# Linear attention, a mixer and a spectral layer on one core: packed copies on SyncE, transposed keys shared between head pairs, and a new written order

## The chip, the core and the metric

The kernel runs on one core of one Trainium2 chip. The metric is the device time of one execution in microseconds (us), from the runs of the program; lower is better. A core has five engines that each run their own instructions in order: TensorE (PE in the profile, with its weight loads as PEld), VectorE (DVE), ScalarE (ACT), GpSimd (POOL) and SyncE (SP), which here issues most transfers. Transfers (DMAs) can be issued by SP, by ACT and by POOL; the profile shows an issue as SPq, ACTq or POOL.

## The reference: what is computed

Three layers follow each other, with B = 4 batches, H = 8 heads, S = 768 tokens, D = 48 per head, and 384 channels.

```python
for t in range(S):                                                       # attention, per batch and head
    state = alpha[:, :, t, :, None] * state + k[:, :, t] (outer) v[:, :, t]
    y[:, :, t] = q[:, :, t] @ state
h = x.T @ U @ V;  u = x + h.T                                            # mixer, rank 32, over tokens
x1 = u + relu(u @ w_ch1) @ w_ch2                                         # 384 -> 1536 -> 384
theta = x1 @ w_theta;  zr, zi = x1 * cos(theta), x1 * sin(theta)         # spectral layer
u = x1 + w_tok_r @ zr + w_tok_i @ zi                                     # 768 x 768 over tokens
out = u + relu(u @ w_ch)
```

The recurrence is computed in chunks of C = 128 tokens (NC = 6 of them): keys and queries are scaled by running products of the decays, the part within a chunk is a masked product of scores and values, and the state between chunks comes from a scan.

## The kernel before, in words

**Layout.** The 384 channels of a batch lie in KD = 3 tiles of 128 rows. A tile i < 3 holds two whole heads (rows 0 to 47 and 64 to 111) and, in rows 48 to 63 and 112 to 127, 16-row pieces of heads 2 and 5 (`ROWS`). Those two heads make the fourth pair (p = 3, `PAIRS[3]`): its keys, queries and decay products are packed out of the three tiles by small transfers, and its results are put back into their rows of X.

**Attention.** `att_load` (SP) loads decays, keys, queries and values. `prep_k` and `prep_q` scale: a DVE scan G (line 247), a product for the keys (249), a second scan (257), a product for the queries (258), and the decay product tp of a chunk (279). `spread` (letter R) calls `spare` (line 239), which packs 16-row pieces of scaled keys into kp and of queries into qp; ACT issues these. `att_pe(b, p)` then makes one pair in eight steps: `across` (transposes of the keys, line 322, copied to kt by ACT, 323), `scores` for two halves (302, with a mask by ACT and POOL, 308 and 309, or by DVE, 312), `increments` (333), `states` (ACT spreads tp into tb, 340, DVE scans into S, 344), `within` (354), `before` (362, copied to X by ACT, 364), and for p = 3 the return of the pieces to X by SP (412).

**Mixer.** Batch 0 goes by `rank_columns` (letters 0, 1, 2; transposes in line 475), the others by `rank` (K; 429, 420). `lift` makes u, split in high and low parts, `expand` and `contract` (M and N, the two halves of the tokens) are the 384-1536-384 layer with three products per tile (598 to 600). The weights arrive as 64-bit words and are decoded by DVE in three passes (`conv`, 511, 514, 517; letters U for U and V, L for w1 and w2, T for the second layer's).

**Spectral layer.** `theta` (H) makes angles, sines and cosines; `factors` (V) and `sums` (S) make the operands of seven token products (terms 2, 1, 6, 7, 5, 3, 4), some of the sums by accumulating transfers from POOL (`plus`, 828); `products7` (G, line 898) makes the products in groups of six matmuls (mx), and adds them to xq (903, 905) after a term's last group; `operands` (Y) and `outputs` (C) end it. `layers`, `back` (X), `squared` (Q, which checks the decays on ACT), `loads` (D), `preps` (P) and `checked` (F) are the other generators; A and B are `products` for even and odd pairs.

**What sets the order.** Everything is issued in a written order: the text `ORDER` is read letter by letter, and each letter runs its generator to its next yield. A generator that needs something not made yet runs the other generator first. The order of the instructions of one engine is the order in which they were issued this way. The strings `BY_K` to `BY_U` say for each of many products, splits and masks whether DVE (V) or POOL (P), or for `BY_A` DVE or ACT with POOL (A), makes it. Tiles in SBUF are `SLOTS` = 61 slots of 128 x 768 words, taken and given back in the written order; PSUM has 8 banks handled alike.

```python
    for x in "".join(ORDER.split()):
        next(gens[x], None)
```

## Time and profile before

| | |
|---|---|
| time, median of 3 runs | 692.6 us (690.29 to 693.17) |
| profiled execution: its own time | 692.24 us |
| profiled execution: span from first to last instruction | 690.5 us |
| mean granted clock of TensorE | 0.984 of full |
| transfers | 71.89 MB, 104 GB/s on the mean |

The span is what the rows below divide. "Busy" is the time in which an engine has at least one instruction running; matmuls overlap each other, so their mean duration is longer than the step from one to the next. "Idle before" and "waits" name what ended a stretch in which an engine had nothing running; a time in square brackets is such a stretch. All window and timeline times count from the start of the span.

### The profile page before, as it was taken

Reading aid. Unit: us, or ns where it says so; the run is one execution under the profiler, and the core shown is the slowest. Engines: PE = TensorE matmul, PEld = TensorE weight load, DVE = VectorE, ACT = ScalarE, POOL = GpSimd, SP = SyncE. Lnnn points to the kernel's source line nnn. Section 1 sums busy time; section 2 is a strip of 40 time slices with the busy share of each in tenths; the row PEclk is TensorE's granted clock in tenths of the full one; section 3 lists DMA queues with packets and bytes.
Section 4 is the critical chain, followed back from the end, with each engine's and each line's share of the span. In section 5 each row is a group of like instructions: output and inputs, shape, how many; then the busy total and the mean of one; then the engine's idle time right before and its main releaser. Section 6 shows DMA issues by size and latency. Waiting matters only on the chain.

```text
span 690.5 us, 11726 instructions
## 1 busy us (share of the span) xinstructions
PE 657.9 (95%) x4658; PEld 627.3 (91%) x4658; DVE 409.3 (59%) x689; ACT 270.1 (39%) x555; POOL 168.7 (24%) x165
## 2 busy tenths in 40 slices
PE   4789999998999999999999999999999979999996
PEld 3687799987888999999999999999999879999996
DVE  7785875783775335443334455677676677885262
ACT  3545542234545331332212452456556443356010
POOL 4524322221323100010000010013625546258100
PEclk9879999999999999999999999999999999999999
DMA  8936544431614123003210021454265954200123
GB/s 298 289 76 213 187 145 137 152 120 42 227 50 135 44 70 92 12 7 116 68 47 1 1 74 40 150 129 112 81 171 97 223 115 115 47 1 35 58 82 108
DMA packets 32576, 71.89 MB, mean 104 GB/s; under 512 B 5056, under 2 KB 12992, under 8 KB 32512
## 3 DMA queue, kind: packets, MB, share of 16 engines
q1 hardware_dynamic: 27264, 60.04, 26.6%
q0 software_dynamic: 3456, 8.26, 6.7%
q10 hardware_dynamic: 1792, 2.76, 1.6%
q8 instruction: 39, 0.64, 0.4%
q14 instruction: 25, 0.20, 0.1%
HBM read 49.40 MB, written 9.44 MB: 85 GB/s over the span
## 4 chain that ended last, share of the span: by engine, by line
PE 78%; DVE 9%; DMA 5%; ACT 3%; issue 2%; ACTq 1%; SPq 0%; POOL 0%; DVEq 0%; POOLq 0%
PE mx L898 15%; PE acc L598 7%; PE h L598 7%; PE acc L600 7%; PE acc L599 7%; PE h L600 6%; PE h L599 6%; PE A L302 3%; PE Y L362 2%; PE th L600 2%; PE ch L598 2%; PE th L598 2%; PE ch L600 2%; PE th L599 2%; PE ch L599 2%
## 5 line engine op out<-in xcount | busy, mean ns | idle before, releaser
L898 PE MATMUL mx<-wp,zh 128*128 128x384 f32 x504 | 129.9, 339 | 3.7 <-DVE xq L905 3.7
L620 DVE SCALAR_TENSOR_TENSOR hh<-h,hh 128x384 fp32r<-128x384 f32 x96 | 52.8, 553 | 107.3 <-ACT hh L619 107.3
L598 PE MATMUL h<-uh,wh 128*128 128x384 f32 x288 | 99.0, 344 | 1.5 <-DVE hh L620 1.5
L619 ACT ACTIVATE hh<-h 128x384 fp32r<-128x384 f32 x96 | 46.7, 490 | 133.8 <-PE h L600 132.9
L598 PE MATMUL acc<-hh,wh 128*128 128x384 f32 x288 | 98.9, 343 | 0.0
L599 PE MATMUL h<-uh,wh 128*128 128x384 f32 x288 | 96.7, 336 | 0.4 <-DVE uh L174 0.2
L600 PE MATMUL acc<-hh,wl 128*128 128x384 f32 x288 | 96.9, 337 | 0.0
L599 PE MATMUL acc<-hh,wh 128*128 128x384 f32 x288 | 96.8, 336 | 0.0
L600 PE MATMUL h<-uh,wl 128*128 128x384 f32 x288 | 96.4, 335 | 0.0
L898 PEld LDWEIGHTS mx<-wp,zh 128*128 128x128 f32 x504 | 91.4, 190 | 4.0 <-ACT zh L173 4.0
L898 PE MATMUL mx<-wp,zl 128*128 128x384 f32 x252 | 84.9, 337 | 0.6 <-DVE zl L174 0.6
L598 PEld LDWEIGHTS h<-uh,wh 128*128 128x128 f32 x288 | 54.1, 188 | 4.7 <-DVE hh L620 2.1
L598 PEld LDWEIGHTS acc<-hh,wh 128*128 128x128 f32 x288 | 54.3, 189 | 1.6 <-issue 0.3
L599 PEld LDWEIGHTS h<-uh,wh 128*128 128x128 f32 x288 | 54.1, 188 | 1.2 <-DVE uh L174 1.2
L599 PEld LDWEIGHTS acc<-hh,wh 128*128 128x128 f32 x288 | 54.4, 189 | 0.0
L600 PEld LDWEIGHTS acc<-hh,wl 128*128 128x128 f32 x288 | 54.3, 189 | 0.0
L600 PEld LDWEIGHTS h<-uh,wl 128*128 128x128 f32 x288 | 54.1, 188 | 0.0
L898 PEld LDWEIGHTS mx<-wp,zl 128*128 128x128 f32 x252 | 47.9, 190 | 0.9 <-DVE zl L174 0.9
L174 POOL TENSOR_TENSOR x1s<-Y,x1s 128x384 fp32r<-128x384 f32 x6 | 6.9, 1174 | 160.0 <-ACT x1s L173 160.0
L309 POOL TENSOR_SCALAR_AFFINE_SELECT Am<-Am 128x384 f32<-128x384 f32 x32 | 20.6, 667 | 66.9 <-ACT Am L308 66.9
L354 PE MATMUL Y<-Am,vv 128*64 128x128 f32 (+1 forms) x384 | 26.9, 290 | 0.5 <-POOL Am L309 0.4
L514 DVE SCALAR_TENSOR_TENSOR cv<-raw,cv 128x384 int32<-128x384 int32 (+2 forms) x39 | 27.0, 717 | 0.3
(212 smaller groups left out, 1237.8 us busy)
## 6 DMA issues: line engine op xcount, KB each, us to landing
raw<-in_w SPq DMA_DIRECT2D x12, 768.0 KB, 5.0
vv<-in_vP SPq DMA_DIRECT2D x16, 291.0 KB, 5.2
raw<-in_wti SPq DMA_DIRECT2D x12, 384.0 KB, 3.6
raw<-in_wtr SPq DMA_DIRECT2D x12, 384.0 KB, 3.7
out<-raw SPq DMA_DIRECT2D x24, 192.0 KB, 1.9
x1d<-X SPq DMA_DIRECT2D x11, 384.0 KB, 3.3
kk<-in_kT SPq DMA_DIRECT2D x10, 384.0 KB, 4.8
qq<-in_qT SPq DMA_DIRECT2D x10, 384.0 KB, 5.7
```

Of the source, the lines that this page charges most:

```text
L174: (e_lo or dve).tensor_tensor(out=lo, in0=src, in1=hi.bitcast(F32), op=ALU.subtract)
L302: pe.matmul(ts[h][:, j * C:(j + 1) * C], k[r, c], q[r, c], start=True, stop=True)
L309: pool.affine_select(out=m, in_=m, pattern=[[0, 3], [1, C]], compare_op=ALU.is_ge, fill=0.0, base=0, channel_multiplier=-1)
L354: pe.matmul(t[64 * h:64 * h + n, o], v[:, c * 96 + h * D:c * 96 + h * D + n], ms[g][h][:, j], start=(j == 0), stop=(c == 0), skip_group_ch ...
L362: pe.matmul(t[64 * h:64 * h + D, o], st[64 * h:64 * h + D, :, c - 1], q[64 * h:64 * h + D, c * C:(c + 1) * C], start=False, stop=True, ski ...
L514: dve.scalar_tensor_tensor(out=t, in0=hi, scalar=-0x40000000, in1=t, op0=ALU.bitwise_and, op1=ALU.bitwise_or)
L598: pe.matmul(out, a[0], b[0], start=first, stop=False)
L599: pe.matmul(out, a[0], b[1], start=False, stop=False)
L600: pe.matmul(out, a[1], b[0], start=False, stop=last)
L619: act.activation(h[:, 0], t[:, 0:HT], ACTF.Relu)
L620: dve.scalar_tensor_tensor(out=h[:, 1], in0=t[:, 0:HT], scalar=0.0, in1=h[:, 0].bitcast(F32), op0=ALU.max, op1=ALU.subtract)
L898: pe.matmul(t[:, 0:HT], x[:, q, c], w[:, y], start=f, stop=l, skip_group_check=True)
```

## The change

- **Packed copies.** `spare` issues its transfers from SP, not ACT, without the 16 rows of padding; `shared` gives (target row, source row) for pieces of 16 rows.
- **Keys of the fourth pair.** It makes no transposes. Each of the other three pairs' `across` copies, besides kt, the 16-row pieces out of its transposed PSUM tile into a tile keys4 of the batch, whose gap columns POOL clears in `prep_k`; the fourth pair's `increments` reads keys4. Its `att_pe` has one step less.
- **Scan in place.** `states` spreads tp into S itself, and the scan reads and writes S; tb goes.
- **Small tiles.** tp becomes 16 tiles, the cleared ones partly later; the three parts of gc become one tile that shares its place with gt; band moves to the small pool. `SLOTS` is 63.
- **Order.** `ORDER` and all `BY_` strings are new. `others` runs the generators 0, 1, 2 to their end ahead of batch 1 rather than batch 3.

```diff
--- before.py
+++ after.py
@@ -25,7 +25,7 @@
 NF = FF // 128
 HT = S // 2
 RANK = 32
-SLOTS = 61
+SLOTS = 63
 LAG = 2
 
 
@@ -37,26 +37,26 @@
 
 
 ORDER = """
-RPPQDARARBADAARBUUQRURUUPABUBBPRUALRPBBAABBAABBQBPBRAABABRPAALABDBA011L20LP2LAAQL1BL22RA02L0L1BLB0RPALA110AL2D
-BMLPMNMAMRLLNQLLAMMLNLNLLNQLNLMLNMLMMMLRNALMLLMLLNMMNMLLMLLMAANNBLPBMLBLTMMDMPNMMANPQPRDBABNBQTPNNBBNABRBBAAPA
-NRKNBBKKNKBKDAKBQDKTBKRNKPBAPRNRBBABKNQBBARPAAAARAABKKABPAAARMAKBRMKMAABBMQTMAMMDPRBMPMABQFTMRAMMMMTKBKAMBBMMK
-TMKBMBMBKANMNANKTTKMNKKXNTMNKBMAKNBNATBBNKNBANNKBNBNTMAMAMNHNNTKKNNBANKMNNMNKMMMMNKKMKNNMMXNKMTNKMKTMMKMKMNMNT
-MTMKMNNFNNMMTNNNNKNNKNHMNNNHTMNKNHHNMFHMHMMHNMHHHKHMKMHMTHMMMMMMTMTMHFMMHMTTTHMNNHTNMTMHHNXTHNHNTTNTHTNHHTHNNH
-VTHHNNTNNHTHTNHHHHNHNNVTTNNVNHTVGNVNVVVVNHHGHHHXHTGGGTGGVHTGGHVVGGGGVVGVVGSVHGGVHVHGHVGSVGSGGVGGGVHVHHGVGGVVGH
-SHVHXHSGGVVGXGVTSGGGVGGGYVGGGGGVVGGGGYSVVGTGVVSVGGGGVGGXGVGVVVGGVGGVGGSGVSVVGGVGGVVGSGGVGVVGGVVVSGGGGGVGVGGGGV
-GVGGGGGVVGVVVYVTTVGGYVVGGGGGGTGGGYGTGGVVVGGVYCGCGVCYGGVCCGGYGVVVVGGGGGVCCVCGGGCGGCYCCGGYCYCCCYCCCCCCCCC
+DRARAPRUQPDURUBURQAPBRBBAPARRPQUABBAAPAUBAUBAALBBBBPAQABBAAAALRLBBLLDLAA0PR022110BLDADL12L201QRBRAL1ALBP02R0L2
+1MALPMMMMBNQLLMALALRLMNLANLMNNLNLLNMLLLMMNLNLMNLNMLLMAMNALBBLMLLLMMLBMLNMPMMPMBMAQPTBDAABAPBANBPRBBTBQRANPANNK
+TQRKNDANNBNRNKKKRKPAKNAPQANBKDAAKARDRABKABAKBRKBPAMBAPBBAMBABAAAMRMMMPKRBMBPMKMMRQQTAMAFTBKMBMMMKMMNTMMRMBKMMT
+AMAMABXBKBNTFTBKBTAFKNNNFNTTNKNBHKNTNBBAKANNNNNBBBNKKBNKKTTNNAANKKNMMKNABKMMKNMNMKNMKMMNMMMMTMMKNKMKXMMKKMTTNN
+MTNKMNNNTMKMNNNMHKNNNTKNNMHNNKNTNHNHMNHKMMNHHMMMHHMHHHMNNMHHMHMHHNHHHTMMNMNTMMHMTTTMNTVNMXMTMHTTHMMVNHTHTHNVTN
+NHVHGTNNTNNHVTTHNNHHHNNHHNNVHHHTTNVNHVHNGGGXVGVHGGHVVHGVTTGTVHGVVGGHGHVGVGVHGSHGGSVGVSHVGGGVVHHGHGVHGVHGGGXVGG
+STVHGVSXGVGGGGGVVGGGGGGVGGVSGVSVSSVGGXVVYGGSSGGGGVVGGGTVGVVGGVVGVGVGVGGGVGVGGVGGGVGGVSVGGVVGGGGVVGVGGGVGGVGVGG
+GGVYGVVGGGVVGVGGYVGGVVYGVYVVGGGVVTGTGVGGGGVTGGGGGVTCGVGVVYGYCGGVCGCYCCGCGCGCCCYGCCGCGCCYCCYYCCCCCCC
 """
 
 
-BY_K = "VVVPVPVVPPVV"
-BY_Q = "VPVPVPPPVPPP"
-BY_W = "PPPVPVPPVVPV"
-BY_A = "VAAAVVVAAVAAVAVVAVAAAAAVVVAAVVVV"
-BY_Z = "PPPPVVVVPVPVPPVVVVVVVVVVPPVVVVPVVVVVVPPPVP"
-BY_X = "PPVPPVVPVVVVVVVPVPVVVVVV"
-BY_T = "PVPPPVPVVPVVVPVPVVPVPVVVVPVVVVVPPPPVVPPPVP"
-BY_U = "VVVPVPPPVVVV"
-BY_S = "VVVVPPVVVVPPPPPPVPVVPVVV"
+BY_K = "VVVPPPVPPVVP"
+BY_Q = "VVVVVPPPVVPV"
+BY_W = "VPVPPPVVPVPP"
+BY_A = "AAVAVVAVAVAAVVAVVVVVVAAAVVVAAVVA"
+BY_Z = "VPVPVVVPPVPPPVVVVVVPVVPVPPVVVVVPPVVVVPPVVP"
+BY_X = "VVVVVPVPVPVPVVVPVVPPVVVV"
+BY_T = "VVPPVVPVVPVVPPVVVVVVVVPVVPVVVVVVVVVVPPVVVP"
+BY_U = "VVVVVPVVPVPP"
+BY_S = "VVVPPPVPPPPVPPVVVVVVPVVV"
 MAGIC = 12582912.0
 INV2PI = 1.0 / (2.0 * math.pi)
 NEG2PI = -6.283185
@@ -150,8 +150,9 @@
     magic = cst.tile([128, 1], F32, name="magic")
     ones = cst.tile([128, 1], F32, name="ones")
     sq = cst.tile([128, B * KD, 2], F32, name="sq")
-    tp = cst.tile([128, B * NP, NC], F32, name="tp")
-    pool.memset(tp, 0.0)
+    tp = [cst.tile([128, NC], F32, name=f"tp{n}") for n in range(B * NP)]
+    for n in (0, KD):
+        pool.memset(tp[n], 0.0)
 
     def more_constants():
         pool.memset(mask, 1.0)
@@ -161,6 +162,9 @@
         pool.memset(minus, -HALFPI)
         pool.memset(magic, MAGIC)
         pool.memset(ones, 1.0)
+        for n in range(1, B * NP):
+            if n != KD:
+                pool.memset(tp[n], 0.0)
         for t in Am:
             pool.memset(t, 0.0)
 
@@ -227,18 +231,17 @@
             sync.dma_start(VV[b, p][:, 0:NC * 97], vP[b * NP + p])
         ld[b, i] = (a, k, q)
 
-    def shared(i, pad=0):
-
-
-        return [(64 * (h == 5) + d, r, n + (pad if (h, d) == (2, 32) else 0)) for h, d, n, r in ROWS[i] if h in PAIRS[KD]]
+    def shared(i):
+
+        return ((32, 48), (96, 112)) if i == 1 else ((32 * i, 48), (32 * i + 16, 112))
 
     def spare(b, i, src, dst, name, x, y):
         if (b, KD) not in dst:
             dst[b, KD] = T(name)
-        for o, r, n in shared(i, 16):
-            act.dma_start(dst[b, KD][o:o + n, x:y], src[r:r + n, x:y])
-
-    moves, moved, wrote = [], [], []
+        for o, r in shared(i):
+            sync.dma_start(dst[b, KD][o:o + 16, x:y], src[r:r + 16, x:y])
+
+    moves, moved, wrote, crossed, keys4 = [], [], [], [], {}
 
     def scale_k(b, i, x, y):
 
@@ -268,6 +271,9 @@
                 scale_k(b, i, x, y)
                 scale_q(b, i, x, y)
         KK[b, i] = pr[b, i][1]
+        if i == 0:
+            keys4[b, KD] = T("kt").rearrange("p (c d) -> p c d", d=128)
+            pool.memset(keys4[b, KD][:, 0:NC - 1, 48:64], 0.0)
 
     def prep_q(b, i):
         if b + i:
@@ -275,11 +281,11 @@
         a, k, q, G = pr.pop((b, i))
         n = b * KD + i
         QQ[b, i] = q
-        tt = tp[:, b * NP + i, 0:NC - 1]
-        dve.tensor_tensor(out=tt.unsqueeze(2), in0=VV[b, i][:, NC * 96 + 1:NC * 97].unsqueeze(2), in1=cols(G, 0)[:, 1:NC],
+        tt = tp[b * NP + i]
+        dve.tensor_tensor(out=tt[:, 0:NC - 1].unsqueeze(2), in0=VV[b, i][:, NC * 96 + 1:NC * 97].unsqueeze(2), in1=cols(G, 0)[:, 1:NC],
                           op=ALU.mult)
-        for o, r, m in shared(i):
-            sync.dma_start(tp[o:o + m, b * NP + KD, 0:NC - 1], tt[r:r + m])
+        for o, r in shared(i):
+            sync.dma_start(tp[b * NP + KD][o:o + 16, 0:NC - 1], tt[r:r + 16, 0:NC - 1])
         if n == B * KD - 1:
             done_with(starts, ends)
 
@@ -315,13 +321,21 @@
             return ms
 
         def across(g):
-            n, m = 3 - g, 128 if p < KD else 112
+            n = 3 - g
             t = PS("kT")
             for j in range(n):
                 c = 3 * g + j
-                pe.transpose(t[:, j * 128:j * 128 + m], k[0:m, c * C:(c + 1) * C], ident[0:m, 0:m])
-            act.copy(kt[:, 3 * g:3 * g + n, 0:m], t[:, 0:n * 128].rearrange("p (c d) -> p c d", d=128)[:, :, 0:m])
+                pe.transpose(t[:, j * 128:(j + 1) * 128], k[:, c * C:(c + 1) * C], ident)
+            act.copy(kt[:, 3 * g:3 * g + n], t[:, 0:n * 128].rearrange("p (c d) -> p c d", d=128))
+            d = keys4[b, KD][:, 3 * g:3 * g + n]
+            if p == 1:
+                d = d.rearrange("p c (a r) -> p c a r", a=2)[:, :, :, 32:48]
+            else:
+                d = d[:, :, 32 * p:32 * p + 32].rearrange("p c (a r) -> p c a r", a=2)
+            act.copy(d, t[:, 0:n * 128].rearrange("p (c a r) -> p c a r", a=2, r=64)[:, :, :, 48:64])
             done_with(t)
+            if g:
+                crossed.append((b, p))
 
         def increments():
 
@@ -336,12 +350,11 @@
 
         def states(t):
 
-            tb = pools["sml"].tile([128, D, NC], F32, tag="tb", name="tb", bufs=2)
-            act.copy(tb, tp[:, b * NP + p].unsqueeze(1).to_broadcast([128, D, NC]))
+            s = pools["sml"].tile([128, D, NC], F32, tag="S", name="S", bufs=2)
+            act.copy(s, tp[b * NP + p].unsqueeze(1).to_broadcast([128, D, NC]))
             dve.memset(t[:, 0:NC * D].rearrange("p (e c) -> p c e", c=NC)[:, NC - 1], 0.0)
-            s = pools["sml"].tile([128, D, NC], F32, tag="S", name="S", bufs=2)
             flat = "p e c -> p (e c)"
-            dve.tensor_tensor_scan(out=s[0:112].rearrange(flat), data0=t[0:112, 0:NC * D], data1=tb[0:112].rearrange(flat),
+            dve.tensor_tensor_scan(out=s[0:112].rearrange(flat), data0=t[0:112, 0:NC * D], data1=s[0:112].rearrange(flat),
                                    initial=0.0, op0=ALU.add, op1=ALU.mult)
             done_with(t)
             return s
@@ -365,11 +378,12 @@
             done_with(t)
 
         ms = []
-        kt = T("kt").rearrange("p (c d) -> p c d", d=128)
-        across(0)
-        if b + p:
-            across(1)
-        yield
+        if p < KD:
+            kt = T("kt").rearrange("p (c d) -> p c d", d=128)
+            across(0)
+            if b + p:
+                across(1)
+            yield
         while (b, p) not in QQ:
             next(gens["P"])
         q = QQ[b, p]
@@ -382,6 +396,11 @@
             next(gens["R"])
         done_with(k)
         yield
+        if p == KD:
+            for i in range(KD):
+                while (b, i) not in crossed:
+                    next(gens["AB"[i % 2]])
+            kt = keys4.pop((b, p))
         dps = increments()
         yield
         st = states(dps)
@@ -408,8 +427,8 @@
             for i in range(KD):
                 while i not in X[b] or b * NP + i not in wrote:
                     next(gens["AB"[i % 2]])
-                for o, r, n in shared(i):
-                    sync.dma_start(X[b][i][r:r + n, :], y[o:o + n, :])
+                for o, r in shared(i):
+                    sync.dma_start(X[b][i][r:r + 16, :], y[o:o + 16, :])
             done_with(y)
         yield 100
 
@@ -482,7 +501,7 @@
             pe.matmul(g[:, 0:128], uv[2][:, o], xs[:, o], start=(s == 0), stop=(s == NC - 1))
         done_with(xs)
         yield
-        gt = pools["sml"].tile([128, 128], F32R, tag="gc", name="gc")
+        gt = gc[:, j * 128:(j + 1) * 128]
         act.copy(gt, g[:, 0:128])
         dve.tensor_tensor(out=gt[96:128], in0=g[96:128, 0:128], in1=gt[96:128].bitcast(F32), op=ALU.subtract)
         done_with(g)
@@ -494,6 +513,7 @@
             yield
 
 
+    gc = pools["sml"].tile([128, 384], F32R, tag="gt", name="gt", bufs=1)
     W1, W2 = [], []
 
     def conv(raw, put):
@@ -1022,7 +1042,7 @@
 
 
     def att_any(xg):
-        band = cst.tile([128, 144], F32, name="band")
+        band = pools["sml"].tile([128, 144], F32, tag="band", name="band", bufs=1)
         pool.memset(band, 0.0)
         pool.memset(band[0:64, 47:48], 1.0)
         pool.memset(band[64:128, 95:96], 1.0)
@@ -1105,7 +1125,7 @@
             if x[0] not in X:
                 X[x[0]] = {}
             for step, _ in enumerate(att_pe(*x)):
-                if step == 7:
+                if step == (7 if x[1] < KD else 6):
                     done.append(n)
                 yield
 
@@ -1144,7 +1164,7 @@
             attended(NP * (b + 1))
             while not uv:
                 next(gens["U"], None)
-            for j in range(KD if b == B - 1 else 0):
+            for j in range(KD if b == 1 else 0):
                 drain(gens[str(j)])
             yield from rank(b)
 
```

## Rows read from the trace of the kernel before

**Rows 1.** The page's first part: busy us, share of the span, instructions

```profile
PE 657.9 (95%) x4658; PEld 627.3 (91%) x4658; DVE 409.3 (59%) x689; ACT 270.1 (39%) x555; POOL 168.7 (24%) x165
```

**Rows 2.** Windows of two stretches: busy us of each engine, clock, DMA share, GB/s

```profile
0.00:75.00 75.00, 58.68 (x605) 49.23 (x605) 53.17 (x78) 35.25 (x82) 32.72 (x48) 0.91 0.71 229
75.00:684.70 609.70, 599.19 (x4054) 578.04 (x4053) 355.61 (x612) 234.90 (x473) 135.98 (x117) 0.99 0.31 89
```

**Rows 3.** Waits of PE: total us, times, longest

```profile
PE mx L898 <- DVE xq L905: 3.7, 1, 3.7
PE kT L322 <- ACT X L364: 3.7, 1, 3.7
...
PE xt L429 <- DMA X<-xp: 2.2, 3, 1.2
...
PE th L598 <- DVE nn L777: 1.0, 1, 1.0
```

**Rows 4.** Windows of the three stretches at the lower clock

```profile
30.40:44.05 13.65, 11.22 (x112) 10.49 (x114) 6.65 (x13) 6.36 (x17) 7.30 (x5) 0.50 0.57 181
163.50:166.90 3.40, 3.40 (x15) 2.97 (x13) 0.56 (x1) 0.63 (x2) 0.00 (x0) 0.50 0.00 0
569.70:573.10 3.40, 3.40 (x11) 3.40 (x12) 3.40 (x7) 1.19 (x2) 3.32 (x4) 0.50 0.85 248
```

**Rows 5.** Groups by line: count, busy us, mean ns, idle before; PE

```profile
L354 PE MATMUL Y<-Am,vv 128*64 128x128 f32 (+1 forms) x384 | 26.9, 290 | 0.5 <-POOL Am L309 0.4
...
L322 PE MATMUL kT<-ident,kp 112*128 112x112 f32 x20 | 3.1, 295 | 3.8 <-ACT X L364 3.7 <-DMA kp<-kk 0.2
```

**Rows 6.** Groups by line, ACT's copies of transposed keys

```profile
L323 ACT COPY kt<-kT 128x384 f32<-128x384 f32 (+3 forms) x30 | 11.0, 430 | 14.7 <-PE kT L322 8.7 <-issue 4.7 <-DMA x1d<-X 1.1
```

**Rows 7.** Timeline of PE, 20 to 50 us: start, us, what, idle before

```profile
22.21 1.34 PE L362 MATMUL Y<-qq,S 48*48 48x128 f32 x20
...
31.71 1.16 PE L322 MATMUL kT<-ident,kp 112*128 112x112 f32 x5 [3.66 <-ACT X L364]
...
47.04 1.26 PE L362 MATMUL Y<-qq,S 48*48 48x128 f32 x20
```

**Rows 8.** Timeline of ACT, 20 to 50 us (ACTq: an issue of transfers)

```profile
24.77 1.99 ACTq L239 DMA_DIRECT2D kp<-kk  x2
...
30.63 0.85 ACT L364 COPY X<-Y 112x384 f32<-112x384 f32 x2
```

**Rows 9.** Timeline of DVE, 15 to 50 us

```profile
17.14 0.76 DVE L344 TENSOR_TENSOR_SCAN S<-D,tb 112x288 f32<-112x288 f32 x1
...
20.41 2.06 DVE L247 TENSOR_TENSOR_SCAN G<-al,ends 128x767 f32<-128x767 f32 x1
22.51 0.96 DVE L249 TENSOR_TENSOR kk<-kk,G 128x767 f32<-128x767 f32 x1
...
25.42 1.76 DVE L257 TENSOR_TENSOR_SCAN al<-al,starts 128x768 f32<-128x768 f32 x1
...
46.98 0.55 DVE L511 TENSOR_SCALAR cv<-raw 128x768 int32<-128x768 int32 x1
```

**Rows 10.** Groups by line, ACT's spread of tp

```profile
L340 ACT COPY tb<-tp 128x288 f32<-128x288 f32 x16 | 6.7, 433 | 1.7 <-issue 1.7
```

**Rows 11.** Instructions that touch xp: ns min/median/max; SP's issues of the returns

```profile
L412 SPq DMA_DIRECT2D X<-xp x18: 507/587/1247, 47.8 to 211.0; - x18
```

**Rows 12.** Timeline of SP, 25 to 60 us: the first loads of W1

```profile
29.86 1.77 SPq L200 DMA_DIRECT2D raw<-in_w  x2
```

**Rows 13.** The page's sixth part: count, KB of one, median us to landing

```profile
raw<-in_w SPq DMA_DIRECT2D x12, 768.0 KB, 5.0
```

**Rows 14.** Timeline of all engines, 155 to 168 us

```profile
156.73 4.34 SPq L412 DMA_DIRECT2D X<-xp  x6
```

**Rows 15.** The chain that ended last, 530 to 575 us: start, us, what

```profile
551.74 6.53 DMA zr<-zr
```

**Rows 16.** Groups by line, wp's low parts on DVE

```profile
L174 DVE TENSOR_TENSOR wp<-cv,wp 128x384 fp32r<-128x384 f32 x21 | 15.4, 735 | 8.3 <-ACT wp L173 8.2
```

## The prediction

> **What bounds the kernel now.** The first part of the page [rows 1] says that TensorE (PE) is busy for 657.9 of 690.5 us and no other engine for two thirds of it. So the end is PE's work plus the time in which PE stands or runs slowly; work on other engines costs only where PE waits for it. Two stretches of the windows [rows 2] say where it stands: 75.00 - 58.68 = 16.3 us in the first 75 us, and 609.7 - 599.19 = 10.5 us from there to the end of the last matmul. The 5.8 us behind that, the last sum and its transfer, the change leaves as they are. The list of PE's waits [rows 3] names the longest ones away from the start: 3.7 for the copies to X, 2.2 for the transfers that return the fourth pair's rows, 1.0 in the angles, 3.7 before the seventh product. The windows of the low clock [rows 4] show the second loss: PE ran at 0.50 (1.2 GHz) in 30.40 to 44.05, in 163.5 to 166.9 and in 569.7 to 573.1, each time after or around one of these waits. PE was busy 11.22, 3.40 and 3.40 us there; at 2.4 GHz that is half, so 5.6, 1.7 and 1.7 us are lost.
>
> **The change part by part.** I followed each letter of both ORDERs (counted from 0) through its generator, which gives what stands ahead of what on each engine.
>
> Transposes. The fourth pair's five transposes per batch go, and with them the wait for its packed keys. They are 20 matmuls, 3.1 us busy [rows 5], of which 0.6 is due to the low clock: 2.5 us off PE.
>
> Copies on ACT. 24 small copies into keys4 come (96 or 64 columns), eight of the fourth pair go. One kt copy takes 430 ns on the mean [rows 6]; the small ones cost between nothing and that, I take 300 ns as they are shorter: 24 x 0.3 - 8 x 0.43 = 3.8 us on an engine that is 39% busy. PE's other work covers it; uncovered, each holds a PSUM bank 0.3 us longer. Four memsets of keys4 and the split of tp go to POOL, 24% busy: nothing.
>
> First stage. The timeline of PE [rows 7] shows the transposes of pair (0,3) at 31.71 after 3.66 us of waiting for X copies, although the `before` matmuls of (0,0) began at 22.21. ACT [rows 8] shows why: the copies (30.63) stand behind two issues of packed keys (24.77, 1.99 us with their wait) and the U and V splits. In the new order the splits come after both pairs' X copies (letter 42 against 35 and 40; before, 32 against 33 and 38), the issues leave ACT, and pair (0,3) asks for no transposes. So the 3.66 can go, and with it the reason for the low clock: 3.66 + 5.6 = 9.3 us at most. What is late next is DVE. Its scan S of (0,0) ran at 17.14 [rows 9]; now the G scan, the product, the second scan and the second product of (0,2) stand ahead (2.06 + 0.96 + 1.76 + 0.96), also q of (0,1), moved from POOL to DVE (0.96), and some 1 us of U's decode: it starts near 24.8 and ends near 25.6. PE arrives at 22.21 plus one `within` moved ahead (26.9 / 16 = 1.7 us [rows 5]), 23.9, and waits 1.7. S of (0,1) follows after another G scan and a decode piece, near 29.4, where PE arrives at 27.7: again 1.7. 9.3 - 3.4 = 5.9 us; `before` of (0,2), which ended at 48.3, should end near 42.4. From there to the first expand PE's list is the same. Bounds: 0 (the low clock comes all the same) and 9.3.
>
> Scan in place, shared tiles. The copy of tp now fills S itself, so it waits for the `before` matmuls of two pairs ago instead of a scan. One copy is 433 ns [rows 10]; in the new order those matmuls stand ahead of it on PE by a whole pair or more. Between 0 and 16 x 0.43 = 6.9 us; I take 0. The gc tile's three parts are all written before the first lift, and rank(1) wants it much later: 0. Two more slots: 0.
>
> Packed copies on SP. 52 issues leave ACT and come to SP. One such issue on SP takes 587 ns (median of the returns [rows 11]). 16 of them now stand ahead of the first W1 load: 9.4 us. That load was issued at 29.86, over 1.77 us [rows 12], lands 5.0 later [rows 13], and its decode starts at 46.98 [rows 9]: 10.3 us of room, so I cost the move at 0. If the room is gone, every us more is one before the first expand. By a sentence of the Trainium skill (DMA: Bandwidth & Descriptors, Anatomy of one DMA) a DMA's semaphore wait is made on the issuing sequencer before dispatch, so a copy whose keys are late holds all the loads behind it on SP; the 1.99 us for two issues on ACT [rows 8] agree with it. By that rule alone the move would cost time, not 0; it is the slower rival below.
>
> Return of the fourth pair, batch 1. SP needs 4.34 us for six returns [rows 14], and the first transposes of X wait 2.2 us for them [rows 3], with the low clock right after. Between the last `before` of the batch and those transposes PE had a kT, two scores and an expand, some 3.8 us at full clock; now a kT, one scores, increments, a contract and two expands, some 6.8. Needed are about 7.2 (two X copies, 4.34, some 2 to land). So 0.4 of 2.2 stays: 1.8 + 1.7 = 3.5 us. Bounds 0 and 3.9.
>
> Late stage. Two thetas in a row cost 1.0 [rows 3]; two mx groups now stand between them: 1.0 gone. Before the seventh product PE waited 3.7 for xq on a DVE that was late because the last sum landed late: issued at 551.74, 6.53 us to landing [rows 15]. From the last theta to that product PE now has 29 groups of 1.04 us in place of 25, and two u2 splits come after it. Against that, the last sum stands 1.0 us of PE's work ahead of the split that reads it, where it was 15.6; with 6.53 to land, that can be a new wait at this spot. 3.7 + 1.7 = 5.4 at most, 0 at least (the wait moves); I take half, 2.7. Eight more low parts of wp on DVE (735 ns each [rows 16], 5.9 us) lie beside mx work: 0, unless DVE is the late one there.
>
> Sum: 2.5 + 5.9 + 3.5 + 1.0 + 2.7 = 15.6 us. The order is new everywhere, so new waits come that no row shows; after 75 us the old order has 10.5 - 2.2 - 1.0 - 3.7 = 3.6 us of small ones, which I leave, and I add somewhat more than as many again, 4.5 (bounds 0 and the 10.5 of all old waits there). 15.6 - 4.5 = 11.1. The profiled execution took 692.24 us, 1.74 more than its span; 692.24 - 11.1 = 681.1, and the median of the runs, 692.6, is 0.4 above it: **681.5 us**. With the terms' ends likely at 676 to 687.
>
> **Rivals.** *All waits go*: every term at its upper end and no new wait, 2.5 + 9.3 + 3.9 + 1.0 + 5.4 = 22.1 us, 670.5; some new waits in it, 670.5 to 675. For it: nearly every named wait has more cover. Against: DVE is busy 53.17 of the first 75 us and its scans now stand closer to PE's needs.
>
> *Waits only change place*: PE's work is the bound, the new order has as many holes as the old one, and only the transposes' 2.5 us are won, 690.1; with scatter 688 to 692. For it: the sum that stands too near its reader, the S scans, the eight wp parts on DVE, and 3.6 us of old small waits. Against: the three longest waits have causes that the new order takes away.
>
> *SP's queue is late* (slower): the first W1 load and what follows are held by packed copies that wait for their keys. 26 copies stand ahead of the first expand's last inputs, 26 x 0.587 = 15.3 us; if all of it shows, the first stage's 5.9 is lost as well, the rest is kept: 692.6 + 15.3 - (15.6 - 5.9 - 4.5) = 702.7, and with half of it 695. It decides once the load lands after about 42 us plus what DVE has to do first. For it: 9.4 of 10.3 us of room are used. Against: the copies' inputs are ready in the order in which SP asks for them.
>
> **How the numbers follow.** The forecast has 0.56, all waits gone 0.13, waits that change place 0.20, SP late 0.11. A measurement of this kernel can tell about 0.5%, 3.5 us, so faster means below 689.1: the first two and a quarter of the third, 0.74; same 0.16 (the rest of the third, and an SP that is only a little late), slower 0.10. For the range I go up to the transposes alone, 690.5, and down into the second case, 673; outside are SP late, some of the third case and the lowest values, about 2 in 10.
>
> **What would show it.** Right: no low clock in 30 to 44 us; `before` of (0,2) ending near 42 us with waits for S of under 2 us each; no low clock near 165; at the seventh product a wait under 3 us. PE's busy time lower by about 10 us, since the low clock counts as busy, with 20 fp32 transposes fewer. Wrong: a wait of PE or DVE for in_w loads in the first 75 us, a low clock in the first stage, ACT standing for S's readers, PE waiting for zh of the last sum, or more than 10 us of new waits after 75 us.

## The result: 673.2 us, and where the time went

Four runs of the kernel after gave a median of 673.18 us (672.23 to 674.07), four of the kernel before on the same chip 691.44 (690.15 to 693.17): a ratio of 0.9734, with a 95% interval of 0.9704 to 0.9764. That is faster and 8.3 us below the forecast; it lies inside the stated range by 0.2 us, which is less than the runs scatter. The profiled execution has a span of 671.5 us, 19.0 less than before.

The page's first part of the kernel after:

```profile
PE 645.9 (96%) x4638; PEld 620.8 (92%) x4638; DVE 422.3 (63%) x702; ACT 270.3 (40%) x567; POOL 155.9 (23%) x171
```

Against [rows 1] PE has 20 matmuls and 12.0 us of busy time less, and two thirds of the gain is there. The windows of the kernel after follow: first its two stretches at the lower clock, then the halves of the span. The columns are the length, the busy time (and instructions) of PE, PEld, DVE, ACT and POOL, the granted clock, the DMA share and GB/s.

```profile
34.14:40.96 6.82, 4.12 (x45) 3.93 (x47) 1.93 (x4) 3.06 (x8) 2.79 (x3) 0.50 0.56 182
75.10:78.51 3.41, 3.41 (x13) 3.41 (x12) 2.65 (x4) 1.41 (x3) 1.67 (x1) 0.50 0.74 222
0.00:75.00 75.00, 56.23 (x615) 48.31 (x616) 59.67 (x86) 40.01 (x99) 26.35 (x62) 0.95 0.72 251
75.00:665.50 590.50, 589.51 (x4025) 572.48 (x4023) 362.12 (x615) 230.33 (x469) 129.55 (x109) 1.00 0.31 88
```

Three things are to be seen against [rows 2, 4]. Behind 75 us PE now stands for 590.50 - 589.51 = 1.0 us, where it stood for 10.5. The two late dips of the clock, near 163 and 570 us, are gone; a new one follows at 75.1. And the first stage still has a low clock, from 34.1 to 41.0, though half as long. The cut at 75 us does not fall on the same work in the two kernels. From the first expand on, which starts at 70.96 in the kernel before (first row) and at 66.89 in the kernel after (second), PE stands for 10.6 and for 2.4 us:

```profile
70.96:684.50 613.54, 602.92 (x4073) 581.16 (x4072) 357.18 (x614) 237.26 (x479) 139.55 (x119) 0.99 0.32 91
66.89:665.50 598.61, 596.21 (x4058) 578.34 (x4057) 367.34 (x624) 233.89 (x477) 129.80 (x110) 1.00 0.31 90
```

The list of PE's waits says what stands there (waited for: us in total, times, longest):

```profile
PE kT L328 <- DVE starts L259: 5.1, 1, 5.1
PE kT L328 <- DVE kk L252: 4.1, 1, 4.1
PE A L308 <- DMA qp<-qq: 3.3, 1, 3.3
PE Y L375 <- DVE S L357: 2.8, 2, 1.4
PE A L308 <- DMA kp<-kk: 0.9, 1, 0.9
PE acc L618 <- ACT hh L639: 0.8, 1, 0.8
...
PE mx L918 <- DVE raw L925: 0.5, 1, 0.5
```

The first two belong to the start and stood there before. None of the four waits of [rows 3] is left at its place. What the prediction calls the seventh product is the product of term 7, the fourth of the seven to run: in the kernel before 324 of the 756 matmuls of the products stand ahead of its wait. The wait of 0.5 us in this list stands one product earlier, behind 216 of them. In the first stage the fourth pair's scores now wait 0.9 us for packed keys and 3.3 for packed queries. PE's timeline of the kernel after (start, us, what, idle before) shows where:

```profile
25.07 1.34 PE L375 MATMUL Y<-qq,S 48*48 48x128 f32 x20 [1.38 <-DVE S L357]
...
28.53 1.34 PE L375 MATMUL Y<-qq,S 48*48 48x128 f32 x20 [1.43 <-DVE S L357]
...
33.04 0.46 PE L308 MATMUL A<-qp,kp 48*128 48x128 f32 x2 [0.92 <-DMA kp<-kk]
36.84 2.90 PE L308 MATMUL A<-qp,kp 48*128 48x128 f32 x22 [3.35 <-DMA qp<-qq]
...
44.76 1.27 PE L375 MATMUL Y<-qq,S 48*48 48x128 f32 x20
```

The last row is `before` of pair (0,2): it ends at 44.76 + 1.27 = 46.0, where it ended at 48.3 [rows 7]. SP's timeline of the kernel after says why those keys and queries came late:

```profile
24.75 0.43 SPq L228 DMA_DIRECT2D qq<-in_qT  x1
25.22 0.43 SPq L231 DMA_DIRECT2D vv<-in_vP  x1
25.70 1.14 SPq L242 DMA_DIRECT2D qp<-qq  x2
26.89 1.22 SPq L242 DMA_DIRECT2D kp<-kk  x2
28.15 1.22 SPq L242 DMA_DIRECT2D qp<-qq  x2
31.09 1.56 SPq L288 DMA_DIRECT2D tp<-tp  x2
32.70 1.22 SPq L242 DMA_DIRECT2D kp<-kk  x2
33.96 1.22 SPq L242 DMA_DIRECT2D qp<-qq  x2
```

Pair (0,2)'s queries were ready on DVE at 24.0, and their issue ended at 35.2. Ahead of it SP issued a whole load of the second batch's second pair (its last two transfers are the first rows here) and the copies of the pairs before, and it stood from 29.4 to 31.1. The list of SP's own waits, for 20 to 40 us, names what for:

```profile
SPq L288 <- DMA qq<-in_qT: 1.6, 1, 1.6
```

That is the transfer issued at 24.75, eight issues ahead of the one that waits. By the trace the waiting issue needs the completion semaphore that this load had used; the load landed at 31.02. So the packed copies were held behind loads on their own queue, though their inputs were there.

### The profile page after: what moved, and what is told of

Same layout as the page of the kernel before. It is cut to its first block, busy times and chain, and to the rows that moved or that the text cites. A ratio compares the mean times of both kernels' runs of the same rounds, so it can differ in the third digit from the quotient of the medians.

```text
span 671.5 us, 11741 instructions
## 1 busy us (share of the span) xinstructions
PE 645.9 (96%) x4638; PEld 620.8 (92%) x4638; DVE 422.3 (63%) x702; ACT 270.3 (40%) x567; POOL 155.9 (23%) x171
## 4 chain that ended last, share of the span: by engine, by line
PE 86%; DVE 6%; DMA 3%; issue 1%; ACT 1%; SPq 1%; DVEq 0%; ACTq 0%
PE mx L918 18%; PE acc L618 8%; PE h L618 8%; PE acc L620 8%; PE acc L619 7%; PE h L620 7%; PE h L619 7%; PE A L308 3%; PE Y L375 2%; PE Y L367 2%; PE ch L618 2%; PE ch L620 2%; PE ch L619 2%; PE th L620 2%; PE th L618 2%; PE th L619 2%
## 5 line engine op out<-in xcount | busy, mean ns | idle before, releaser
L918 PE MATMUL mx<-wp,zh 128*128 128x384 f32 x504 | 128.4, 335 | 0.5 <-DVE raw L925 0.5
L178 POOL TENSOR_TENSOR x1s<-Y,x1s 128x384 fp32r<-128x384 f32 x2 | 2.0, 1009 | 127.3 <-ACT x1s L177 127.3
L315 POOL TENSOR_SCALAR_AFFINE_SELECT Am<-Am 128x384 f32<-128x384 f32 x28 | 16.3, 611 | 62.0 <-ACT Am L314 62.0
L177 ACT CAST zh<-zr 128x768 fp32r<-128x768 f32 x23 | 19.2, 833 | 23.3 <-DVE zr L885 9.4
```

The costliest lines, as they stand in the source:

```text
L177: act.copy(hi, src)
L315: pool.affine_select(out=m, in_=m, pattern=[[0, 3], [1, C]], compare_op=ALU.is_ge, fill=0.0, base=0, channel_multiplier=-1)
L918: pe.matmul(t[:, 0:HT], x[:, q, c], w[:, y], start=f, stop=l, skip_group_check=True)
```

## The experiments

Ratios are to runs of the kernel before that were made beside each experiment (their medians were 692.2 to 692.9 us), so the experiments can be compared with each other. Four things change together: the order of steps, the engine strings (the BY lines, which say for each operation whether VectorE or GpSimd, or ScalarE, does it), the queue of the 52 packed copies, and the data flow of the fourth pair. The rest, the scan in place, the small tiles and the two slots, was not taken apart from these.

### New parts, old order

The kernel after with ORDER and all BY strings of before. An empty step of the fourth pair is kept, so that each letter means what it meant:

```diff
-DRARAPRUQPDURUBURQAPBRBBAPARRPQUABBAAPAUBAUBAALBB...
+RPPQDARARBADAARBUUQRURUUPABUBBPRUALRPBBAABBAABBQB...
-BY_K = "VVVPPPVPPVVP"
+BY_K = "VVVPVPVVPPVV"
...
-            yield
+        yield
```

> The changed kernel with the order and the engine strings of the kernel before (the fourth pair keeps an empty step so that the letters fit). Theory 'order' (the waits went because the letters stand elsewhere): only the 20 transposes and at most the 3.66 us wait for X copies go, 685 to 691 us, and the low clock near 163 us and near 570 us is still there. Rival 'parts' (the gain is made by the data flow: no packed keys to transpose, no issues on ACT): below 679 us, the waits near 160 and 565 us gone.

Measured: 699.55 us (697.1 to 700.26), ratio 1.0102 (1.0074 to 1.0131), slower than before and outside every expectation. First the wait in PE's list that grew, then the windows of its two longest stretches at the lower clock:

```profile
PE A L308 <- DMA qp<-qq: 10.7, 2, 7.6
```

```profile
30.75:47.82 17.07, 9.44 (x103) 8.76 (x101) 7.57 (x14) 3.18 (x8) 5.48 (x5) 0.50 0.32 107
187.76:201.42 13.66, 12.62 (x115) 10.94 (x117) 4.84 (x7) 4.89 (x13) 2.98 (x6) 0.50 0.28 103
```

The 7.6 us wait ended at 41.17, and its queries had been issued on SP from 34.79 to 35.93, right behind two loads of weights (33.63); they landed at 40.98. The second, of 3.1 us, is that of the second batch; ahead of those queries SP (its list for 170 to 190 us) stood before a copy of decay products whose input was late:

```profile
SPq L288 <- DVE tp L285: 6.1, 1, 6.1
```

The low clock goes with both waits. The rival "SP's queue is late" did come about here.

### The same, copies issued by ScalarE

```diff
-            sync.dma_start(dst[b, KD][o:o + 16, x:y], src[r:r + 16, x:y])
+            act.dma_start(dst[b, KD][o:o + 16, x:y], src[r:r + 16, x:y])
```

> The kernel parts_alone (new parts, order and strings of before) with the 52 packed copies issued by ScalarE again, so that against the kernel before it has the transposed keys from the other pairs' tiles and the scan in place. Theory 'late queue': parts_alone was slow because SP reached the packed queries late (10.7 us of waits, 30 us at the low clock); on ScalarE these go: 685 to 690. Rival 'order': the old order doesn't suit the new parts wherever the copies are issued: 695 to 702.

Measured: 689.09 us (684.9 to 691.74), ratio 0.9944 (0.992 to 0.9967). The second batch's wait for queries and its low clock at 187.8 are gone. The first batch's wait is shorter but not gone, and the low clock there lasts 13.65 us, as in the kernel before:

```profile
PE A L308 <- DMA raw<-in_w: 4.3, 1, 4.3
```

The row names a load of weights, which these scores do not read. By the trace they wait for the semaphores of the queries that ScalarE had issued at 30.39 and 31.81; these landed at 35.35 and 37.78, beside the weights. So in the old order SP's queue cost about 1.6% (1.0102 against 0.9944), 7.0 of the 9.9 us of span behind the first expand, and the tiles put together from the others, with the scan in place and the small tiles, were worth 0.6%, some 4 us.

### Copies on ScalarE, with everything else of after

The same line in the kernel after.

> The changed kernel with the 52 packed copies issued by ACT again. Theory 'order' with SP as the late queue of the first stage (PE waited 3.35 us for packed queries whose issue stood on SP behind loads): that wait and part of the low clock after it go, 667 to 672 us. Rival 'the move off ACT made the gain': ACT's PSUM copies come late as before, 678 us or more.

Measured: 681.58 us (680.23 to 686.63), ratio 0.9876 (0.9831 to 0.9922), as the rival said. The same move that cost 1.6% with the old order brings 1.4% with the new one. The 4.2 us of waits for packed keys and queries are gone, yet the first expand starts 2.6 us later, at 69.5. Two waits of PE are longer than in the kernel after, where they are 2.8 and 0.8 us:

```profile
PE Y L375 <- DVE S L357: 5.7, 2, 3.8
...
PE acc L618 <- ACT hh L639: 2.5, 1, 2.5
```

ACT's timeline shows the first: the spread of pair (0,1)'s increments, on which that scan depends, starts at 31.66, where it was 25.68 in the kernel after, behind two pairs of issues.

```profile
26.95 1.16 ACTq L242 DMA_DIRECT2D kp<-kk  x2
28.53 1.42 ACTq L242 DMA_DIRECT2D qp<-qq  x2
...
31.66 0.41 ACT L354 COPY S<-tp 128x288 f32<-128x288 f32 x1
```

### The old data flow in the new order, on either queue

The kernel after with the fourth pair's own transposes, padded copies, no keys4 (core of the edit, with copies on ScalarE):

```diff
-        for o, r in shared(i):
-            sync.dma_start(dst[b, KD][o:o + 16, x:y], src[r:r + 16, x:y])
+        for o, r, n in shared(i, 16):
+            act.dma_start(dst[b, KD][o:o + n, x:y], src[r:r + n, x:y])
...
-            act.copy(d, t[:, 0:n * 128].rearrange("p (c a r) -> p c a r", a=2, r=64)[:, :, :, 48:64])
...
+        kt = T("kt").rearrange("p (c d) -> p c d", d=128)
+        across(0)
+        if b + p:
+            across(1)
...
-            kt = keys4.pop((b, p))
```

> The changed kernel with its order, engine strings, slots and in-place scan, but the data flow of before: the fourth pair packs its keys with padding, ACT issues the copies, and the pair makes its own 20 transposes; no copies into keys4. Theory 'order': 673 plus about 2 us of transposes plus at most 5 us of waits for packed keys, 675 to 680 us. Rival 'parts': 684 us or more.

Measured: 682.69 us (681.94 to 684.44), ratio 0.9866 (0.9845 to 0.9886), between the two expectations. Order, strings, slots, small tiles and scan bring 1.3% with no change to the copies' queue. Then the same with `sync` for `act`:

> The kernel old_flow (order, strings, slots and scan in place of after; padded copies, 20 transposes and own copies of the keys for the fourth pair as before) with the packed copies issued by SP instead of ScalarE. Against after it lacks only the transposed keys from the other pairs' tiles. Theory 'flow small': the 20 transposes cost the 2.5 us that the prediction put on them, the move to SP brings the 8 us that it brought with the new flow: 674 to 677.5. Rival 'flow carries': the move to SP pays only together with the tiles that are put together from the others, since the 80 more copies stay on ScalarE: 679 to 684.

Measured: 674.83 us (674.32 to 675.29), ratio 0.9749 (0.9719 to 0.9779). The move to SP brings 1.2% here too, and the shared tiles hardly any more than the runs resolve: 0.9749 to 0.9734 on SP, 0.9866 to 0.9876 on ScalarE.

### The engine strings

The kernel after with all nine strings of before (BY_K is shown, the others follow the same pattern):

```diff
-BY_K = "VVVPPPVPPVVP"
+BY_K = "VVVPVPVVPPVV"
...
```

> The changed kernel with all engine strings (which of DVE, POOL, ACT makes a product, split or mask) of the kernel before. Theory 'order': 672 to 678 us. Rival 'engine choices' (queries of the first batches on DVE, eight more low parts of wp on DVE): 682 us or more, with new waits in the first 75 us and in the products.

Measured: 682.08 us (681.26 to 683.71), ratio 0.9864 (0.9839 to 0.9889). PE's list has the old wait before term 7's product again, and a dip of the clock at 558.8 us behind it:

```profile
PE mx L918 <- DVE xq L925: 3.9, 1, 3.9
```

What PE waits for is not an operand ("quantised input" in the recorded expectations is wrong). VectorE adds the finished sum of the product ahead out of PSUM to xq (line 925), and term 7's product goes on summing in the same PSUM tile. VectorE's and GpSimd's timelines of this kernel show what holds that addition: two of the sums that make the products' operands (line 877) run on each engine at the same time.

```profile
552.54 3.71 DVE L877 TENSOR_TENSOR cv<-cv 128x384 f32<-128x384 f32 x2
...
558.52 2.87 DVE L925 TENSOR_TENSOR xq<-mx,xq 128x384 f32<-128x384 f32 x6
```

```profile
552.90 2.94 POOL L877 TENSOR_TENSOR cv<-cv 128x384 f32<-128x384 f32 x2
```

The same two timelines of the kernel after have one sum on VectorE, then three on GpSimd:

```profile
545.10 0.55 DVE L877 TENSOR_TENSOR cv<-cv 128x384 f32<-128x384 f32 x1
```

```profile
545.81 3.27 POOL L877 TENSOR_TENSOR cv<-cv 128x384 f32<-128x384 f32 x3 [3.67 <-DVE cv L877]
```

Alone a sum takes VectorE 0.55 us, so the two beside GpSimd's lost 3.71 - 1.10 = 2.6 us. The addition to xq stands behind them. Counted from the start of the product ahead (536.41 here, 534.35 in the kernel after, where the addition starts at 551.27) it comes 22.1 us in and not 16.9, so 5.2 us later. These two sums are half of that. Another 1.8 us are a transfer (zr<-raw), which GpSimd issues here behind a sum of its own and ScalarE's split waits for; the rest is not put down to a row.

Then only the five strings that act behind the first 75 us, as before:

> The kernel after with five of its nine engine strings (the splits of weights, quantised inputs, transposed activations and sums, all used behind the first 75 us) as before; keys, queries, low halves of the weights and the triangle's copies stay new. Theory 'late': about half of the 9 us that all nine strings were worth lies at the seventh product: its wait on the quantised input (3 to 4 us) and a stretch of 3.4 us at the low clock come back: 676.5 to 679.5. Rival 'early': the 9 us lie in the first 75 us (the triangle's copies and the queries on GpSimd): 672 to 675.

Measured: 680.16 us (679.83 to 680.67), ratio 0.9823 (0.9783 to 0.9862), just above the band of 'late'. Most of the 9 us lies at these five: the wait of 3.3 us is back, with 6.8 us at the lower clock behind it. Then the reverse, the kernel before with the nine new strings:

> The kernel before with the engine strings of the kernel after, nothing else. Theory 'strings': the strings are a gain of their own, the wait of the seventh product for its quantised input (3.7 us) and the 3.4 us at the low clock behind it go: 685 to 688.5. Rival 'fit': the strings belong to the new order, and in the old one they lengthen other steps as much as they shorten this one: 690 to 697, with the wait still there or another of 3 us or more in its place.

Measured: 696.31 us (692.33 to 699.18), ratio 1.0049 (1.0026 to 1.0072). The strings alone make the old order a little slower. The wait before term 7's product is gone here too, but PE's list shows a longer one, for another tile, before the product ahead of it (behind 216 matmuls of the products):

```profile
PE mx L898 <- DVE raw L905: 5.5, 1, 5.5
```

So of the four pairings of orders and strings the two with the old strings have the wait at term 7 (3.7 and 3.9 us) and the two with the new strings do not. What the new strings put in its place one product earlier is 5.5 us in the old order and 0.5 in the new one.

### What holds the first stage

Only the first batch's copies on ScalarE:

```diff
-            sync.dma_start(dst[b, KD][o:o + 16, x:y], src[r:r + 16, x:y])
+            (sync if b else act).dma_start(dst[b, KD][o:o + 16, x:y], src[r:r + 16, x:y])
```

> The kernel after with the packed copies of the first batch issued by ScalarE, all others by SP. Theory 'SP late': the two waits for packed keys and queries (0.9 and 3.3 us) and most of the 6.8 us at the low clock go: 667 to 671. Rival 'ScalarE late': the issues (0.6 us each) hold up ScalarE's copies of states and outputs between 20 and 40 us, and the wait for the scan of states grows from 1.4 to 3 us or more, as where ScalarE issued all: 673 to 682.

Measured: 675.64 us (674.77 to 676.81), ratio 0.9761 (0.9719 to 0.9802), hardly to be told apart from the kernel after (its four runs lie just above, the intervals overlap). PE's waits for packed keys and queries go, 4.1 us for the triangle's copies and 2.8 for one scan of states come, and the 6.8 us at the lower clock become two stretches of 3.4, from 24.9 and from 45.4: the wait changes place.

Next, leave the copies on SP and take a load from ahead of them. One letter of the order moves, D at position 10 goes behind the third pair's copies:

```diff
-DRARAPRUQPDURUBURQAPBRBBAPARRPQUABB...
+DRARAPRUQPURUBURQAPBRBBAPARRDPQUABB...
```

> The kernel after with one letter of the order moved: the load of the second batch's second pair (issued by SP from 23.65 to 25.65 us) comes behind the packed copies of the first batch's third pair. Theory 'held by loads': SP came late to these copies since the load's four issues stood ahead of them and its queue then waited for earlier loads at 29.4 to 31.1 us; now the copies of the queries are issued 2 to 3.5 us earlier, the wait of 3.3 us shrinks to below 1.5, and the low clock between 34 and 41 us goes or halves: 668 to 671.5. Rival 'queries ready': the queries themselves (ready on VectorE at 31.8 us) and the 1.2 us that each pair of issues takes set the landing, so that nothing moves: 672 to 674.5. Third: the load lands too late for its scans, and waits of 2 us or more come behind 42 us: 674.5 to 679.

Measured: 669.65 us (668.61 to 670.88), ratio 0.9684 (0.9658 to 0.971), all five runs below all four of the kernel after. SP's timeline of this kernel: the copies go out in one row, 3.7 us earlier, and the load follows them. (In the kernel after the load's four issues took 2.0 us and the stand behind them 1.7.)

```profile
27.80 1.15 SPq L288 DMA_DIRECT2D tp<-tp  x2
29.00 1.22 SPq L242 DMA_DIRECT2D kp<-kk  x2
30.26 1.22 SPq L242 DMA_DIRECT2D qp<-qq  x2
31.52 0.58 SPq L228 DMA_DIRECT2D al<-in_aT  x1
```

Its window of 30 to 45 us, and PE's timeline in it:

```profile
30.00:45.00 15.00, 13.09 (x210) 11.62 (x210) 12.27 (x19) 10.07 (x25) 7.13 (x7) 1.00 0.76 239
```

```profile
34.51 1.57 PE L308 MATMUL A<-qp,kp 48*128 48x128 f32 x22 [1.90 <-ACT v L608]
...
40.71 1.34 PE L375 MATMUL Y<-qq,S 48*48 48x128 f32 x20
```

The clock stays at 1.00, the two waits together are 1.9 us where they were 4.2, and `before` of pair (0,2) ends at 40.71 + 1.34 = 42.05. (The row names ScalarE's v as the last to come. By the trace the scores wait for the semaphores of the two packed copies of queries as well, and these landed at 34.09 and 34.27, 3.8 and 3.4 us after their issue, just ahead of the start at 34.51.) Against the kernel after that is 4.0 us earlier, and the span is 4.6 shorter. Of the two theories the one that says "held by loads" has it; the rival's 31.8 us is the time of another pair's queries, these were ready at 24.0 in the kernel after. The first expand starts 3.0 us earlier, and the dip at 75.1 is gone too, which is 1.7 more. Two waits of 0.8 and 0.4 us in the first contract stand 2.5 and 1 us ahead of that dip in the kernel after; load_later has the same two without a dip, so what decides it is not shown.

The other load of the second batch moved as well (D at position 0 to where the first one stood):

> As load_later, and the load of the second batch's first pair (SP, 14.6 to 17.8 us) comes four steps later, where the other one stood. Theory 'held by loads': the packed keys go out earlier as well, the wait of 0.9 us goes too: 667 to 671. Rival 'too late': its pair's scan at 41.9 us or the triangle behind it gets its data late and PE waits as much there as it gains here: 672 to 678.

Measured: 670.78 us (670.0 to 671.42), ratio 0.9693 (0.9667 to 0.9719), the same as load_later within the interval. The keys do go out at 14.8 instead of 18.4, but what stands last at the scores stays 2.0 us. Two stretches of 3.4 us at the lower clock are back, from 35.7 and from 73.2.

Last, the tenth pair of copies of load_later on ScalarE:

```diff
-            sync.dma_start(dst[b, KD][o:o + 16, x:y], src[r:r + 16, x:y])
+            (act if (b, i, name) == (0, 2, "qp") else sync).dma_start(dst[b, KD][o:o + 16, x:y], src[r:r + 16, x:y])
```

> The kernel load_later with one more pair of transfers moved: the last packed queries of the first batch are issued by ScalarE, where they stand ahead of two squares, instead of as the tenth pair in a row on SP. Theory 'issue queue': what is left of the wait in the fourth pair's scores (1.9 us at 32.6 us) is SP's ten pairs of issues at 1.2 us each; on ScalarE these queries go out near 24 to 25.5 us instead of 30.3 to 31.5, the wait goes, and every later load is 1.2 us earlier on SP: 666.5 to 669. Rival 'ScalarE holds': the two issues push ScalarE's spread of states, output copies and transposed keys back by 1.2 us, and PE waits for these as long as it gains: 669.5 to 672.

Measured: 673.04 us (672.71 to 674.68), ratio 0.9722 (0.9707 to 0.9737), worse than load_later and right for neither theory. These queries did leave at 24.08, and ScalarE held nobody, but SP did. Its list of waits (10 to 40 us), ACT's and SP's timelines:

```profile
SPq L242 <- DMA qp<-qq: 3.6, 1, 3.6
```

```profile
24.08 1.23 ACTq L242 DMA_DIRECT2D qp<-qq  x2
```

```profile
20.70 1.92 SPq L242 DMA_DIRECT2D qp<-qq  x2
26.22 1.14 SPq L242 DMA_DIRECT2D kp<-kk  x2
```

SP stood with the first pair's keys, which do not need that transfer, until the queries that ScalarE had issued were in place: by the trace its issue at 26.22 takes over the semaphore of ScalarE's issue at 24.08, which landed at 26.20. The copies behind it leave some 5 us later than in load_later, and the low clock is back (30.1 to 33.5 and 36.9 to 43.7 us).

## Why the prediction was right, and where its terms were not

The sign held by a wide margin, the range by 0.2 us, so that the time fell inside it was luck: one of the four runs lies below 673. The time lies in the band of "all waits go", which had a chance of 0.13. Of the signs named for "right", those of the late stages came true (no dip near 165, a wait under 3 us at the seventh product, PE's busy time lower by 12.0 us where about 10 was said), those of the first stage only in part; and a low clock in the first stage, one of the signs named for "wrong", came as well. The span fell by 19.0 where 11.1 was forecast; by its own terms:

**Transposes**, 2.5 us. Twenty fp32 matmuls less are in the page. The edit as a whole, with the copies that it needs, was worth 0.6% in the old order and 1 us or so in the new, not resolved there: the size is borne out no closer than between 0 and 5 us.

**First stage**, 5.9 us, `before` of (0,2) at 42.4. Measured: 46.0, so 2.3 of 5.9 at that point; the first expand starts at 66.9, 4.1 earlier than before. The two steps that I took from DVE held: the scans of states began at 24.3 and ended at 28.5 (24.8 and 29.4 forecast) and PE waited 1.4 us for each (1.7). The step that failed is "I cost the move at 0". It asked only when SP reaches the first load of W1, and that load came in time. It did not ask when SP reaches the copies themselves, behind the loads. The runs show the price: with the one load out of the way `before` ends at 42.05 and no low clock is left, as forecast; the hold cost 4.0 us at that point and 3.0 at the first expand. The rule named beside this term (the Trainium skill, DMA: Bandwidth & Descriptors, Anatomy of one DMA: a DMA's wait is made on the sequencer that issues it) agrees with SP's 1.6 us stand and, in parts_alone, with the second batch's queries. As a rival it had the right mechanism with the wrong victim, and in the new order the move gains more than the hold costs: 1.4% against copies on ScalarE.

**Return of the fourth pair, batch 1**, 3.5 us. None of its 2.2 us of waits and no dip is left: 3.9, the upper bound. **Two thetas**, 1.0: gone, as forecast.

**Seventh product**, 2.7 us (half of 5.4). The wait and the dip are gone, so all 5.4 came; the 0.5 us one product earlier is a new wait. My half rested on PE's 29 groups ahead of it and on a last sum that might come late. The runs show that the order does not decide it: with the new order and the old strings the wait is 3.9 us, with the old order and the new strings it is gone. The engine strings decide, five of them for 3.3 us of it, and I priced only BY_T's eight low parts, at 0. That it is the sums' engine (BY_S) among the five is read from the timelines; that string alone was not tried. What the order does decide is the wait that the new strings bring one product earlier: 5.5 in strings_alone, 0.4 in old_flow, which differs from it in order, scan, slots and small tiles alone.

**New waits**, -4.5 us, and 3.6 of small old ones left. This is the term that was mis-sized most. From the first expand on PE stands for 2.4 us in all, not 8.1, and the new dip at 75.1 adds 3.41 / 2 = 1.7: 4.0 us better than forecast, half of the miss. The order was counted as a source of holes in proportion to its size; here order, strings and queue together closed most of them: with the old strings 8.8 us are left from the first expand on, with the copies on ScalarE 6.0.

Put together: 11.1 - 2.4 (first stage by the first expand: 5.9 and 0.6 for the first batch's transposes were forecast, 4.1 came) + 0.4 (return) + 2.7 (seventh product, the 0.5 being counted in the 2.4) + 4.0 = 15.8 of 19.0 us. The last 3.2 lie in PE's busy time and not in its holes: behind the first expand it is 602.92 - 596.21 = 6.7 us less, of which 15 transposes are 1.9 and one dip less 1.7. No run shows which instructions the rest is.

"Waits only change place" describes two of the experiments (first_on_act, strings_alone) but not the change. "All waits go" is what its time came close to, though the first stage kept some: part of it lies in the busy time that no term had.

Left open: the scan in place, the small tiles and the two slots alone; the order alone, with the old strings, data flow and queue; whether another order would win as much without the move to SP.

## What to carry to other kernels

An order written out by hand, the engine of each step and the queue of each transfer fit each other: the same move to SP cost 1.6% in one order and brought 1.4% in another, and new engine strings cost 0.5% alone and brought 1.3% with their order. So price such an edit as one, and test it by pairs, not by undoing one part at a time: the losses from undoing the queue, the strings and the data flow (1.4, 1.3 and 0.2%) already make up the whole 2.7%, with the order not counted. When small transfers are moved onto a queue that also carries loads, count what stands ahead of each of them on that queue and ask which load is not yet due: one letter of the order, a load moved behind them, gave the best kernel here, 669.65 us.

## What the runs showed of the hardware that I had not expected

- An issue can stand for a transfer that it has no use for: on SP for 1.6 us at 29.4 (the transfer issued eight ahead), and for 3.6 us in last_q_act for one that ScalarE had issued. The trace has the reason: the issues of SP and ScalarE share eight completion semaphores, given out in turn, and each issue goes out only when the transfer that last used its semaphore has landed (in all 276 cases of the kernel after, GpSimd's own eight counted in). In the first row that is the load issued at 24.75, landed at 31.02, and the issue went out at 31.09; in the second ScalarE's of 24.08, landed at 26.20, and SP's went out at 26.22. A version with more of them was not tried.
- Two issues of 16 rows take 1.2 us of SP, whether a row has 384 or 768 elements, so the ten pairs that stand in a row in load_later, with those of the decay products, take from 18.43 to 31.48 us, in which nothing else leaves that queue.
- A sum of 128 x 384 took 0.55 us on VectorE alone; two took 3.71 us while GpSimd did two of its own.
